# A chunked RWKV-7 recurrence with a hash-routed expert layer: the first group's triangular inverse in 16-row blocks

## The chip, the cores and the metric

The kernel runs on one core of a Trainium2 chip. The metric is the device time of one execution in microseconds. Before the change three runs took 639.33, 641.83 and 646.64 us, median 641.83.

A core has five engines that run at the same time, each through its own list of instructions and in order: TensorE (PE in the profile, with PEld for its weight loads), VectorE (DVE), ScalarE (ACT), GpSimd (POOL) and SyncE (SP). TensorE writes its results to eight banks of PSUM, from which VectorE and ScalarE copy them to SBUF. SP, POOL and ACT issue DMA transfers.

## The reference

There are two parts. The first is a recurrence over 768 steps for each of 4 x 8 heads, with a 40 x 40 state for each head:

```python
for t in range(S):
    y[:, :, t] = np.einsum('bhd,bhde->bhe', rt, state)
    Sa = np.einsum('bhde,bhe->bhd', state, at)
    state_decay = state * wt[:, :, None, :] - np.einsum('bhd,bhe->bhde', Sa, bt)
    state = state_decay + np.einsum('bhd,bhe->bhde', vt, kt)
```

The state starts at zero. The second part takes y as 3072 rows of 320 and sends each row through one of 8 experts, chosen by a hash of the row's token: `np.maximum(xe @ w1[e], 0.0) @ w2[e]`. All is in float32.

## The kernel before

The recurrence is worked out in chunks of 64 steps. A tile is one chunk of two of the four batches (16 heads), and there are 24 tiles. Inside a chunk the steps depend on one another through a strictly triangular 64 x 64 matrix for each head, built from a, b and the decays; the kernel inverts (identity minus this matrix) explicitly. For each tile u there are two halves.

- The scores (`tile_a`), at tick u. VectorE multiplies a, b and k with products of decays (`at`, `z`), TensorE turns these (`z_ps`, `t_ps`) and multiplies them (`a_ps`). VectorE masks one half of `a_ps` (`mk`). ScalarE copies the other half: the two 32 x 32 blocks on the diagonal to `pk`, the block beside them to `no`.
- The state step (`tile_s`, `tile_m`, `tile_b`), eight ticks later (`LAG`). It takes the inverse (`um`), the state and v to the new rows (`r1_ps`, `nc_ps`, `x_t_ps`, `rc_ps`), the next state (`s_ps`, `sd_ps`) and the output (`y_ps`).

In between, four tiles make a group, and `group_i` inverts the 32 x 32 blocks of the whole group at once on VectorE, with the elements of 128 matrices on 128 partitions. After a transpose (L613) come 30 steps, one for each column: a product into `outer` (L632) and its sum into `nu` (L639), of 32 to 272 elements on each partition, each needing the one before. Two transposes (L647, L648) bring the result back as `ut` and `ug`. `tile_m` then makes each tile's 64 x 64 inverse from the two inverted blocks: TensorE multiplies `no` with one of them (`x_ps`), ScalarE copies it and the blocks themselves (`xi`, `um`), TensorE multiplies with the other (`u_ps`), and ScalarE copies that to its place.

The decays come in six rounds of four tiles each (`decays`): products over w by levels on VectorE (L384, then `spread`, L393 and L395), stored to DRAM through SP's queue (L355) as p and q, and loaded again for each tile through POOL's queue (`ql`, `pl`).

The order on every engine is written out by hand. Each piece of work has a place on a scale of ticks (`at_tick`), and the list is sorted by it; inside a tick 14 steps have names (`STEPS`). The program then waits wherever data or buffers need it. For the scores of tiles 4 to 6 `LATE` gives fractions of a tick by which they come later. All matmuls go through one helper, L307, so the profile names them by their tiles. PSUM is shared by six buffers: four of one bank (`bank`) and two of two banks (`two_banks`); `z_ps`, `a_ps`, `nc_ps`, `x_t_ps`, `rc_ps` and `sd_ps` all take turns on the two.

The states live in three forms: `st`, and two copies of it in the layouts that the products need (`sb` and `sd`), filled with zeros by ScalarE at ticks 4.2, 4.9 and 5.9 and written after every state step.

## Time and profile before

One execution was profiled. It took 640.76 us, of which the profile spans 638.6.

| engine | busy us | share of the span |
|---|---|---|
| PE | 558.6 | 87% |
| PEld | 424.1 | 66% |
| DVE | 352.2 | 55% |
| ACT | 295.5 | 46% |
| POOL | 196.0 | 31% |

The recurrence takes about the first half: `a_ps` of the last tile starts at 303 us. The rest is the expert layer, which the change does not touch. Of the recurrence, the first 88 us build up: the decays of rounds 0 to 2, the scores of tiles 0 to 7 and the inversion of the first group. Then the state steps begin, and each later tick is one tile's scores with another tile's state step.

A line of a timeline has the start, the length from the first start to the last end, the engine, the line of the program, the operation, what it writes and reads, its shape and how many instructions are merged; in brackets stands how long the engine was idle before it and what ended that. A line of a table by stage has the window, its length, and then busy time and number of instructions of PE, PEld, DVE, ACT and POOL, TensorE's granted clock (1.00 is full speed), the DMA engines' mean busy share, and GB/s.

### The profile page before, as it was taken

To read this page: it belongs to the slowest core of one execution; us is meant where nothing else is said; L and a number is where in the kernel's file an instruction comes from. 1 tells how busy PE (TensorE), PEld (TensorE's weight loads), DVE (VectorE), ACT (ScalarE), POOL (GpSimd) and SP (SyncE) were. 2 spreads that over 40 slices of the span, in tenths; PEclk is the share of its full clock that TensorE was granted. 3 is DMA by queue.
4 is the path that set the end of the run, shared out by engine and by line. 5 is a ranking of instruction groups with operands and counts; after the bars stand their busy time and mean duration, and the time that the engine had idled before them with its cause. 6 is when DMAs were issued, how large, how long until landed. Compare 5 with 4: busy or idle time off the path is not lost.

```text
span 638.6 us, 22953 instructions
## 1 busy us (share of the span) xinstructions
PE 558.6 (87%) x9866; PEld 424.1 (66%) x9866; DVE 352.2 (55%) x920; ACT 295.5 (46%) x695; POOL 196.0 (31%) x331
## 2 busy tenths in 40 slices
PE   0443678899989999999999998999999999999995
PEld 0432667788878887888888887756565646565552
DVE  6878879768968986887797443132022112303010
ACT  4162457667767877778675751014042213101110
POOL 0621351425333345333231321461313132130101
PEclk9985579899999999999999999999999999999998
DMA  9999997978898797732435614695334273220000
GB/s 160 192 205 170 178 180 120 192 136 156 177 159 153 138 184 151 134 87 58 107 67 113 148 45 147 198 329 192 111 104 132 96 259 106 88 82 12 31 12 25
DMA packets 195769, 85.12 MB, mean 133 GB/s; under 512 B 176718, under 2 KB 186191, under 8 KB 195664
## 3 DMA queue, kind: packets, MB, share of 16 engines
q1 hardware_dynamic: 184016, 45.59, 37.5%
q0 software_dynamic: 11456, 37.37, 20.3%
q8 instruction: 78, 1.28, 0.8%
q10 hardware_dynamic: 192, 0.66, 0.4%
q14 instruction: 27, 0.22, 0.1%
HBM read 66.54 MB, written 15.40 MB: 128 GB/s over the span
## 4 chain that ended last, share of the span: by engine, by line
PE 42%; issue 22%; DVE 16%; DMA 5%; SPq 5%; POOL 4%; ACT 4%; POOLq 0%; DVEq 0%; ACTq 0%
PE up_ps L1077 6%; PE dn_ps L1095 6%; PE y_ps L307 4%; PE s_ps L307 3%; PE rc_ps L307 3%; SPq L326 3%; PE a_ps L307 3%; DVE mr L762 3%; PE x_t_ps L750 2%; DVE outer L632 2%; POOL out_dram L1100 2%; PE sd_ps L810 2%; DVE nu L639 2%; PE nc_ps L307 2%; PE x_ps L307 2%
## 5 line engine op out<-in xcount | busy, mean ns | idle before, releaser
L1085 DVE TENSOR_SCALAR ht<-up_ps 128x416 f32<-128x416 f32 (+2 forms) x36 | 19.4, 543 | 165.1 <-PE up_ps L1082 163.5
L1095 PE MATMUL dn_ps<-w,ht 128*128 128x320 f32 x336 | 91.7, 433 | 0.0
L1077 PE MATMUL up_ps<-xt,w 128*128 128x416 f32 x224 | 81.3, 516 | 0.0
L1095 PEld LDWEIGHTS dn_ps<-w,ht 128*128 128x128 f32 x336 | 63.3, 190 | 25.5
L1100 POOL DMA_INDIRECT out_dram<-o,idx_all x26 | 26.1, 1004 | 166.3 <-ACT o L1099 164.8
L802 POOL DMA_DIRECT2D x_rows<-xs x44 | 23.2, 535 | 164.5 <-DVE xs L798 56.9
L1087 ACT ACTIVATE ht<-up_ps 128x416 f32<-128x416 f32 (+2 forms) x36 | 17.2, 479 | 107.4 <-PE up_ps L1082 107.4
L1077 PEld LDWEIGHTS up_ps<-xt,w 128*128 128x128 f32 x224 | 41.9, 190 | 36.9 <-issue 31.7
L632 DVE TENSOR_TENSOR outer<-nu 128x252 f32<-128x252 f32 (+8 forms) x180 | 63.5, 353 | 5.3
L639 DVE TENSOR_TENSOR nu<-nu,outer 128x252 f32<-128x252 f32 (+8 forms) x180 | 63.2, 351 | 4.6
L1099 ACT COPY o<-dn_ps 128x320 f32<-128x320 f32 x26 | 11.1, 426 | 92.5 <-PE dn_ps L1095 92.5
L537 PE MATMUL z_ps<-ident,z 128*104 128x128 f32 x192 | 31.9, 319 | 20.0 <-DVE z L523 17.2
L541 ACT COPY z_t<-z_ps 104x512 f32<-104x512 f32 x48 | 25.8, 590 | 38.8 <-PE z_ps L537 37.6
L740 ACT COPY x<-nc_ps 64x320 f32<-64x320 f32 x48 | 20.2, 420 | 50.5 <-PE nc_ps L307 49.9
L484 POOL DMA_DIRECT2D ql<-q_rows x48 | 25.1, 531 | 50.0 <-DVE pb L393 15.8
L537 PEld LDWEIGHTS z_ps<-ident,z 128*104 128x104 f32 x192 | 25.1, 152 | 22.8 <-issue 18.8
L762 DVE TENSOR_TENSOR mr<-rc_ps,after 128x1024 f32<-128x1024 f32 x24 | 29.3, 1219 | 13.3 <-PE rc_ps L307 13.3
L307 PE MATMUL rc_ps<-r_t,x_t 64*64 64x64 f32 x1536 | 29.6, 222 | 7.4 <-DVE mk L564 4.3
L307 PE MATMUL a_ps<-at_t,z_t 64*64 64x64 f32 x1536 | 31.5, 237 | 3.6 <-ACT at_t L590 2.7
L307 PEld LDWEIGHTS rc_ps<-r_t,x_t 64*64 64x64 f32 x1536 | 25.5, 134 | 12.5 <-DVE mk L564 8.8
L564 DVE TENSOR_TENSOR mk<-a_ps,after 128x512 f32<-128x512 f32 x24 | 16.5, 689 | 30.7 <-ACT no L581 26.6
L307 PEld LDWEIGHTS a_ps<-at_t,z_t 64*64 64x64 f32 x1536 | 27.9, 149 | 6.4 <-ACT at_t L590 3.9
(230 smaller groups left out, 1127.8 us busy)
## 6 DMA issues: line engine op xcount, KB each, us to landing
ql<-q_rows POOLq DMA_DIRECT2D x48, 160.0 KB, 4.1
w<-in_moe_w_dram SPq DMA_DIRECT2D x10, 640.0 KB, 7.4
w<-in_moe_w_dram SPq DMA_DIRECT2D x10, 512.0 KB, 4.7
al<-in_a_dram SPq DMA_DIRECT2D x48, 80.0 KB, 4.4
pl<-p_rows POOLq DMA_DIRECT2D x48, 80.0 KB, 4.5
r<-in_r_dram SPq DMA_DIRECT2D x48, 80.0 KB, 3.6
x<-in_v_dram SPq DMA_DIRECT2D x48, 80.0 KB, 3.2
py<-p_rows POOLq DMA_DIRECT2D x48, 80.0 KB, 4.3
```

Of the source, the lines that this page charges most:

```text
L307: nc.tensor.matmul(out_, lhsT=lhsT, rhs=rhs, start=start, stop=stop, skip_group_check=True)
L484: nc.gpsimd.dma_start(ql[half(be)], of_batches(rows_of_chunk("q"), 2 * g, 2))
L537: nc.tensor.transpose(p[0:R, be, hp * P:(hp + 1) * P], x["z"][:, be, hp, :], ident[:])
L541: nc.scalar.copy(t[0:R, be].rearrange("p h t -> p (h t)"), p[0:R, be])
L632: nc.vector.tensor_tensor(tv, paired(x["u"])[:, 0:full[1], j:j + 1, :].to_broadcast(full), paired(x["n"])[:, j // 2, j + 1:, j % 2].unsque ...
L639: nc.vector.tensor_tensor(o, o, x["t"][:, 0:n].rearrange("p (c i k) -> p c i k", c=full[1], k=2), op=OP.add)
L740: nc.scalar.copy(x["x"][half(be), be].rearrange("p (a q) (two e) -> p a (q two) e", a=2, two=2)[:, :, :, 0:D], p[half(be), :, 0:HP * D].re ...
L762: nc.vector.tensor_tensor(t[:].rearrange("p two h t -> p (two h) t"), p[:].rearrange("p two (h t) -> p (two h) t", t=C), after[:].unsqueez ...
L802: dma(x_of[2 * g + be, n * C:(n + 1) * C], xs[half(be), :])
L1077: nc.tensor.matmul(p[:], lhsT=w1[c][:, (f0 + i) * P:(f0 + i + 1) * P], rhs=xt[:, c, 0:n], start=(c == 0), stop=False)
L1095: nc.tensor.matmul(p[i * m:(i + 1) * m], lhsT=ht[:, f, c0:c0 + m], rhs=w2[f // (FP // 2)][:, f % (FP // 2), :], start=(f == 0), stop=(f == ...
L1100: st = nc.gpsimd.indirect_dma_start(out=out[:], out_offset=bass.IndirectOffsetOnAxis(ap=idx, axis=0), in_=o[0:m], in_offset=None, bounds_c ...
```

## The change

For the first group alone, the explicit inversion on VectorE goes by blocks of 16 rows: 14 steps, not 30, each of two products (one for each of two pairs of blocks) and one sum. The rest of each 64 x 64 matrix, that is the three 16-row strips beside the four inverted blocks, is kept whole in `off` (a fill and three scaled copies by ScalarE, in place of the copy `no`). `tile_m16` takes the place of `tile_m` for tiles 0 to 3. It multiplies `off` with the inverted blocks on TensorE (`mt_ps`), copies that to `mt` and the blocks to `um`, and then forms um + mt x now three times in series, now being um first and then the last result: each time one product with the identity, 16 products of 64 x 64 and a copy by ScalarE (`sum_ps`). These pieces stand at ticks 5.3, 6.12 and 6.92 for tiles 0 to 2 and 10.22 for tile 3, with 0.2 ticks between them.

`off` and, for tiles 0 and 1, `um` are kept in the buffers of `sb` and `sd`, which are cleared later (ticks 7.55 to 10.3). Since these states are empty in the first chunk, the products with them (`r1_ps` and `y_ps` for tiles 0 and 1) are left out. The buffer of `mt` is one of the two of `wt`, the loaded decays. The places of tiles 4 to 6's scores move later, and so do the spreads and stores of the decays of round 2 and the load of round 3. In the sorted order this puts, on TensorE, the products of tile 0 between `z_ps` and `a_ps` of tile 5, those of tile 1 before `a_ps` of tile 6, and those of tile 2 before `a_ps` of tile 7; on VectorE the spreads of round 2 come behind the inversion of group 0; on SP the stores of round 2 and the load of round 3 come directly before the first loads of r and v and before the loads of tile 8. The other groups are inverted as before, by the same code under a new name (`by_columns`).

The diff, cut to its core:

```diff
-    sb_r, sd_r = (ring(n, NG, [P, 2, HP, 2, D], all_of, i) for n, i in (("sb", 4.9), ("sd", 5.9)))
+    states = [hold.tile([P, 2, HP, 2, D], F32, name=f"s{n}{i}") for n in "bd" for i in range(NG)]
+    sb_r, sd_r = ((lambda u, ts=ts: ts[u % NG]) for ts in (states[:NG], states[NG:]))
+    for i, t in enumerate(states):
+        at_tick((8.25, 9.25, 7.55, 10.3)[i])(lambda t=t: clear(t[:]))
+    def lent(u):
+        return states[u][:].rearrange("p b hp two d -> p (b hp two d)")[:, 0:HP * 2 * C].rearrange("p (h t) -> p h t", t=C)
...
+    HB = BLK // 2
+    above = hold.tile([P, 3], F32, name="above")
+    nc.vector.memset(above[:], 0.0)
+    for be in range(2):
+        for i in range(3):
+            nc.vector.memset(above[be * C:be * C + (i + 1) * HB, i:i + 1], 1.0)
...
-    LATE = {4: 0.45, 5: 0.3, 6: 0.15}
+    LATE = {4: 0.6, 5: 0.4, 6: 0.2}
...
-            x["no"] = no = work.tile([P, 2, HP, BLK], F32, tag="no", name="no", bufs=LAG)
+            if not ahead:
+                x["no"] = no = work.tile([P, 2, HP, BLK], F32, tag="no", name="no", bufs=LAG)
             nc.scalar.copy(pk, of_k(of_b[:, :, :, 0:BLK]))
             for i in range(2):
                 nc.scalar.copy(pk[low(i)], of_k(of_b[low(i), :, :, BLK:C]))
-            nc.scalar.copy(no[:], of_b[:, :, :, BLK:C])
+            if not ahead:
+                nc.scalar.copy(no[:], of_b[:, :, :, BLK:C])
+            else:
+                x["off"] = off = lent(u)
+                nc.scalar.copy(off[:, :, 0:HB], zero[:].unsqueeze(1).to_broadcast([P, H, HB]))
+                for i in range(3):
+                    cols = slice((i + 1) * HB, (i + 2) * HB)
+                    nc.scalar.activation(off[:, :, cols].rearrange("p (two h) t -> p two h t", two=2), of_b[:, :, :, cols],
+                                         AF.Copy, scale=above[:, i:i + 1])
...
+        if gi == 0:
+            dt = (t2 - t1) / (2 * HB - 3)
+            def sub(v, row, col, dims, q=None):
+                step = HB // 2 * 2 * BLK + HB * 2
+                return bass.AP(v.tensor, v.offset + row // 2 * 2 * BLK + col * 2 + row % 2 + (q or 0) * step,
+                               [v.ap[0], *([(step, 2)] if q is None else []), *dims])
+            @at_tick(t1, order=9)
+            def _():
+                nc.vector.tensor_copy(sub(x["u"], 0, 1, [(2, HB - 1)]), sub(x["n"], 0, 1, [(2, HB - 1)]))
+            for j in range(1, HB - 1):
+                m, c = HB - 1 - j, j // 2 + 1
+                @at_tick(t1 + dt * (2 * j - 1), order=9)
+                def _(j=j, m=m, c=c):
+                    x["t"] = work.tile([P, BLK * BLK // 4 + BLK // 2], F32, tag="outer", name="outer", bufs=1)
+                    tv = x["t"][:, 0:4 * c * m].rearrange("p (q c i k) -> p q c i k", q=2, c=c, k=2)
+                    for q in range(2):
+                        nc.vector.tensor_tensor(tv[:, q], sub(x["u"], 0, j, [(2 * BLK, c), (0, m), (1, 2)], q),
+                                                sub(x["n"], j, j + 1, [(0, c), (2, m), (0, 2)], q), op=OP.mult)
+                @at_tick(t1 + dt * 2 * j, order=9)
+                def _(j=j, m=m, c=c):
+                    o = sub(x["u"], 0, j + 1, [(2 * BLK, c), (1, 2 * m)])
+                    tv = x["t"][:, 0:4 * c * m].rearrange("p (q c i) -> p q c i", q=2, c=c)
+                    nc.vector.tensor_tensor(o, o, tv, op=OP.add)
+        else:
+            by_columns(x, t1, t2)
...
+    def mt_buffer():
+        groups[0]["mt"] = early.tile([P, HC * D], F32, tag="wt", name="mt", bufs=2)[:, 0:4 * HP * C].rearrange(
+            "p (two h t) -> p two h t", two=2, t=C)
+    at_tick(8.9)(mt_buffer)
+    def tile_m16(u, t0):
+        x = tiles[u]
+        @at_tick(t0)
+        def _():
+            ut, ug = (paired(groups[0][n])[:, u * H // 2:(u + 1) * H // 2] for n in ("ut", "ug"))
+            if u == 0:
+                mt_buffer()
+            both = groups[0]["mt"]
+            x["mt"], x["sum"] = mt, _ = both[:, 0], both[:, 1]
+            p = two_banks("mt_ps")
+            for par, be, hp in heads_of("par", "be", "hq", "al"):
+                h, a = hx(par, be, hp), al(hp)
+                for i, rows in enumerate((top(a), low(a))):
+                    mm(p[half(a), i, h * BLK:(h + 1) * BLK], x["off"][rows, h, :], ut[rows, h // 2, :, h % 2])
+            nc.scalar.copy(mt.rearrange("p h (two t) -> p two h t", two=2),
+                           p[:, :, 0:H * BLK].rearrange("p two (h t) -> p two h t", t=BLK))
+            x["um"] = um = lent(u) if u < 2 else work.tile([P, H, C], F32, tag="um", name="um", bufs=1)[:]
+            for i in range(2):
+                nc.scalar.activation(um[:, :, i * BLK:(i + 1) * BLK].rearrange("p (g k) t -> p g k t", k=2),
+                                     ug.rearrange("p g t k -> p g k t"), AF.Copy, scale=first[:, i:i + 1])
+        for i, f in enumerate((0.2, 0.4, 0.6)):
+            @at_tick(t0 + f)
+            def _(i=i):
+                mt, um = x["mt"], x["um"]
+                now = x["sum"] if i else um
+                p = bank([P, H, C], "sum_ps")
+                mm(p.rearrange("p h t -> p (h t)"), ident[:], um.rearrange("p h t -> p (h t)"), stop=False)
+                for par, be, hp in heads_of("par", "be", "hq", "al"):
+                    h, a = hx(par, be, hp), al(hp)
+                    mm(p[half(a), h, :], mt[half(a), h, :], now[half(a), h, :], start=False)
+                nc.scalar.copy(um if i == 2 else x["sum"], p)
     def tile_m(u, t0):
 
         x = tiles[u]
         gi, ti = divmod(u, GRP)
         x_order = ("par", "be", "hq", "al")
+        if gi == 0:
+            return tile_m16(u, (5.3, 6.12, 6.92, 10.22)[u])
...
-            for _, be, hp in heads_of("hq", "be", "al"):
+            for _, be, hp in heads_of("hq", "be", "al") if n else ():
...
-            for _, be, hp in heads_of("hp", "be"):
+            for _, be, hp in heads_of("hp", "be") if n else ():
...
-    decays(2, 0.86, 2.7, 0.2, (3.0, 3.01, 3.02, 3.66, 3.67, 4.0, 4.3, 4.31))
+    decays(2, 0.86, 2.7, 0.2, (3.0, 3.01, 3.02, 5.26, 5.27, 5.4, 5.41, 5.42))
...
-        decays(ri, t0 - 2.1, t0, 0.12, [t0 + f for f in (0.86, 0.92, 0.921, 1.0, 1.3, 1.86, 2.0, 1.31)])
+        decays(ri, t0 - (1.5 if ri == 3 else 2.1), t0, 0.12, [t0 + f for f in (0.86, 0.92, 0.921, 1.0, 1.3, 1.86, 2.0, 1.31)])
...
-        group_i(gi, t0 + 0.05, t0 + (0.33 if last else 0.1), t0 + (3.44 if last else 3.4))
+        group_i(gi, t0 + 0.05, t0 + (0.33 if last else 0.1), t0 + (3.44 if last else 3.4 if gi else 1.6))
```

More of the change, by code (lines that the diff above doesn't have):

```diff
@@ L596, in paired, with by_columns, place_of @@
         return t.rearrange("p (i j k) -> p i j k", i=BLK // 2, k=2)
-    def group_i(gi, t0, t1, t2):
-        x = groups[gi]
-        @at_tick(t0 - 0.5, order=9)
-        def _():
-            x["nu"] = nu = early.tile([P, 2, BLK * BLK], F32, tag="nu", name="nu")
-            x["n"], x["u"] = nu[:, 0], nu[:, 1]
-            ub = x["u"]
-            nc.gpsimd.memset(ub, 0.0)
-            nc.gpsimd.memset(bass.AP(ub.tensor, ub.offset, [ub.ap[0], (2 * BLK + 4, BLK // 2), (3, 2)]), 1.0)
-        @at_tick(t0, order=9)
-        def _():
-            nc.vector.transpose(paired(x["n"]).rearrange("p s t k -> p t s k"), paired(x["pk"]).rearrange("p t h k -> p t k h"))
+    def by_columns(x, t1, t2):
         dt = (t2 - t1) / (2 * BLK - 3)
-        place_of = (lambda t: max(t1, by_time(t))) if gi else (lambda t: t)
+        def place_of(t):
+            return max(t1, by_time(t))
         @at_tick(t1, order=9)
@@ L639, in _, with group_i @@
                 nc.vector.tensor_tensor(o, o, x["t"][:, 0:n].rearrange("p (c i k) -> p c i k", c=full[1], k=2), op=OP.add)
-        @at_tick(place_of(t2), order=9)
+    def group_i(gi, t0, t1, t2):
+        x = groups[gi]
+        @at_tick(t0 - 0.5, order=9)
+        def _():
+            x["nu"] = nu = early.tile([P, 2, BLK * BLK], F32, tag="nu", name="nu")
+            x["n"], x["u"] = nu[:, 0], nu[:, 1]
+            ub = x["u"]
+            nc.gpsimd.memset(ub, 0.0)
+            nc.gpsimd.memset(bass.AP(ub.tensor, ub.offset, [ub.ap[0], (2 * BLK + 4, BLK // 2), (3, 2)]), 1.0)
+        @at_tick(t0, order=9)
+        def _():
+            nc.vector.transpose(paired(x["n"]).rearrange("p s t k -> p t s k"), paired(x["pk"]).rearrange("p t h k -> p t k h"))
+        if gi == 0:
[5 more added lines that the diff above has]
+            @at_tick(t1, order=9)
+            def _():
+                nc.vector.tensor_copy(sub(x["u"], 0, 1, [(2, HB - 1)]), sub(x["n"], 0, 1, [(2, HB - 1)]))
[15 more added lines that the diff above has]
+            by_columns(x, t1, t2)
+        @at_tick(max(t1, by_time(t2)) if gi else t2, order=9)
@@ L648, in _ @@
             nc.vector.transpose(paired(ug).rearrange("p g t k -> p t g k"), ub.rearrange("p s t k -> p t s k"))
+    def mt_buffer():
[5 more added lines that the diff above has]
+        @at_tick(t0)
+        def _():
+            ut, ug = (paired(groups[0][n])[:, u * H // 2:(u + 1) * H // 2] for n in ("ut", "ug"))
[25 more added lines that the diff above has]
+                nc.scalar.copy(um if i == 2 else x["sum"], p)
     def tile_m(u, t0):
@@ L725, in _ @@
                 mm(p[half(al(hp)), par, hp % HQ * 2:hp % HQ * 2 + 2, :], x["mk"][:, par, hp, :], x["x"][:, :, hp, par * C:par * C + D],
-                   start=False)
+                   start=n == 0 and par == 0 and hp % HQ == 0)
             x["r1"] = r1 = r1_r(u)
@@ L795, in _ @@
                 mm(p[half(be), c0:c0 + D], x["mr"][:, par, hp * 2 + be, :], x["z"][:, be, hp, par * C:par * C + D],
-                   start=False)
+                   start=n == 0 and par == 0 and hp == 0)
             xs = work.tile([P, DM], F32, tag="xs", name="xs")
```

## The prediction

> **What bounds the kernel now.** I read the busy shares in 40 slices first, then the engines by stage, then the timelines of VectorE, TensorE and ScalarE from 25 to 145 us, and the chain of waits for the same time. The change touches only the first group, so the question is what sets the pace before the loop of tiles is full.
>
> ```profile
> PE   0443678899989999999999998999999999999995
> DVE  6878879768968986887797443132022112303010
> PEclk9985579899999999999999999999999999999998
> ```
>
> A slice is 16 us. In slices 3 to 5 TensorE (PE) is half idle at a low clock and VectorE (DVE) is full; from slice 6 on TensorE is full. By stage (busy us, then the clock and the DMA share):
>
> ```profile
> 57.70:67.20 9.50, 4.76 (x76) 4.18 (x76) 8.09 (x19) 4.29 (x10) 3.09 (x6) 0.50 0.96 165
> 98.10:112.40 14.30, 12.49 (x376) 10.77 (x370) 13.78 (x33) 10.16 (x25) 1.99 (x5) 1.00 0.77 128
> 130.50:143.10 12.60, 12.48 (x374) 10.87 (x370) 9.94 (x27) 9.50 (x23) 2.26 (x4) 1.00 0.71 117
> ```
>
> The third number group is VectorE: 8.1 of 9.5 us while group 0 is inverted, 13.8 of 14.3 while group 1 is, and 9.9 of 12.6 later, where TensorE (first group) is the full one. The exact borders come from the timelines. VectorE:
>
> ```profile
> 46.81 1.24 DVE L613 STREAM_TRANSPOSE nu<-pk 128x1024 f32<-128x1024 f32 x1
> ...
> 81.62 1.25 DVE L647 STREAM_TRANSPOSE ut<-nu 128x1024 f32<-128x1024 f32 x1
> ...
> 90.05 0.69 DVE L564 TENSOR_TENSOR mk<-a_ps,after 128x512 f32<-128x512 f32 x1 [2.48 <-ACT no L581]
> 90.66 1.24 DVE L613 STREAM_TRANSPOSE nu<-pk 128x1024 f32<-128x1024 f32 x1
> ...
> 115.82 0.68 DVE L564 TENSOR_TENSOR mk<-a_ps,after 128x512 f32<-128x512 f32 x1
> ```
>
> Group 0 takes VectorE from 46.8 to 84.0. The scores of tiles 4 to 7 lie inside it; those of tile 7 end at 88.4 and its mask at 90.66. There group 1 begins, and from 90.66 to the mask of tile 9 (116.4) VectorE has no listed wait: 25.8 us that its own order sets. After that TensorE sets the pace to the end of the loop. So one number carries the forecast: **when tile 7's mask is done**, 90.66 now. All behind it moves with it.
>
> **What goes.** Of group 0's 60 column operations (L632, L639; in all 63.5 + 63.2 us over six groups, 21.1 for one, 22.9 with 0.03 between two) 42 small ones stay. Rows: 60 elements take 0.22, 272 take 0.44, so about 0.16 + 0.001 an element; two independent ones overlap by 0.08 (L384: 0.48 long, 0.39 apart). A step has two products of 16 to 72 elements and one sum of twice that: 0.13 + 0.25 + 0.305 = 0.69 on average, 14 steps 9.6 us. Bounds: 14 x 3 x 0.19 (the smallest row) = 8.0 and, without overlap, 11.3. VectorE saves about 13 us. Also gone for tiles 0 to 3 are x_ps, u_ps and their copies, r1's state half and y's state half for tiles 0 and 1 (0.77 each), and one 0.37 copy "no" per tile.
>
> **What comes on ScalarE and VectorE early.** "no" becomes a fill and three scaled copies of 128x128: between 0.25 and 0.35 each by the 0.30 apart of 128x192 copies (L205); I take 0.26, so +0.7 a tile. Each a_ps buffer is free that much later; two of these lie on the chain, and mk of tile 3 goes from 44.07 to 45.5. But the 2.1 us of L393 between it and the transpose move behind the inversion, so the transpose needs only tile 3's pk copies: 47.4 against 46.81. Inversion begins at 49.05; six steps 4.2; at and z of tile 4 1.15 (their data landed by 52.3); eight steps 5.4: 59.8. at and z of tile 5 follow, to 61.0. Tile 4's scores on cold TensorE: z_ps 54.5, t_ps, a_ps 58.05 to 60.05; copies 1.55, mk to 62.35. Then the ut transposes, the first done at **63.6 against 82.9**. That is the gain: 19 us.
>
> **What is put in its place.** TensorE is in order, and the products of tile 0 stand before a_ps of tile 5, those of tile 1 before a_ps of 6, those of tile 2 before a_ps of 7. So the saved time does not reach tile 7 unless the products are short. Rows for them:
>
> ```profile
> 96.12 0.70 PE L307 MATMUL s_ps<-st,ident 104*104 104x320 f32 x2
> 96.75 0.81 PE L307 MATMUL s_ps<-x,z 128*40 128x40 f32 x32
> 97.50 0.69 PE L307 MATMUL u_ps<-um,xi 32*32 32x32 f32 x32
> 98.12 1.16 PE L307 MATMUL a_ps<-at_t,z_t 64*64 64x64 f32 x64
> ```
>
> The identity product has 512 columns: 0.63 x 512/320 = 1.0 us. Its 16 products of 64x64 are half of a_ps: 0.57 (0.69 by u_ps). One stage **1.57 us** at full clock, bounds 1.46 (up_ps has 0.87 ns a column) and 1.81. Behind each stage is a ScalarE copy of 128x512 with handover, 0.65, which the next one needs: three in series, nothing of the same tile beside them. mt_ps is 32 products, 64 records: 64/32 x 0.69 = 1.38, bounds 1.16 (a_ps) and 2.26 (y_ps, 1.13 for 32). Copy 0.6 and um 0.95 (L669) must end before the first stage.
>
> mt_ps also needs a two-bank buffer. There are two: z_ps of the next tile takes one, and the other is a_ps of the tile before, free after its mask. So one tile runs, from the end of an a_ps: 1.65 for pk and no, 0.7 mk, 1.4 mt_ps, 0.6 + 0.95, 3 x 1.57 + 2 x 0.65 = 6.0, some 0.1 in handovers, a_ps 1.16: **12.55 us**. z_ps and t_ps lie in its gaps. Now it is 9.2 to 10 (a_ps at 57.7, 67.2, 76.4, 86.4), even at half clock.
>
> Sum: mt_ps of tile 0 63.65 to 65.75 (cold, 2.1), um done 67.3, first stage 2.4 while the clock rises, 69.75; second 71.95; third 74.2; a_ps of tile 5 ends 75.35. Two cycles of 12.55: a_ps of tile 7 ends at 100.45, its mask 2.3 later (as now): **102.75 against 90.66, +12.1 us**.
>
> **Behind it.** Group 1's 25.8 us on VectorE keep the same operations in the same order, so TensorE's savings there (x, u and r1's half, 2 to 3 us) are not seen. After tile 9's mask TensorE leads:
>
> ```profile
> 120.83 0.66 PE L307 MATMUL nc_ps<-r,um 64*64 64x40 f32 x28
> 123.12 0.44 PE L307 MATMUL nc_ps<-r,um 64*64 64x40 f32 x4 [1.63 <-issue]
> 123.49 1.06 PE L307 MATMUL x_ps<-ut,no 32*32 32x32 f32 x32
> ```
>
> There TensorE stops 1.63 us and then runs at half clock until 129: with the durations of the next tick nc to a_ps would be 4.9 us, not 9.05. Tile 3's mt_ps and stages come in just here: mt 1.24, wait for um 0.85, sum 1.57, x_t and s 2.25, sum 1.57 and sd in between make 8.2 from nc's end, third stage 1.57 after a_ps. If the stop does not come back this tick ends 0.7 later than now; if it does, up to 4.5 more. Total **+12.8**: 640.76 + 12.8 = 653.6, so **654**. The profiled execution (span 638.6, 2.2 around it) is 1.1 under the median 641.83 of runs from 639.33 to 646.64, and I leave it there.
>
> **Transfers.** Round 2's stores (4.2 and 5.6 us on SP) move from 60 to behind the inversion, and round 3's w behind them. Issued from about 67 they end near 77; w and r, v and tile 8's loads follow to 87. Tile 8's z is due only after tile 6's mask, near 94, so this costs nothing; without the long TensorE chain it would be up to 10 us late, another reason why a fast chain would not give its whole gain. The states are filled later on ScalarE, 0.7 each, beside TensorE's work: nothing. Round 4's w now waits for round 3's and holds SP's queue (r, v and q stores behind it) some 5 us; r_t there is due 13 us later, so nothing, at worst 5.
>
> **The clock, weighed apart.** In the row, 1.6 us of stop at 121.5 is enough for 0.50 from 123 on, and 4.7 us of work (76.4 to 81.1) lift it. The Trainium skill (TensorE: Matmul & The Clock Gate, "What's actually happening") says that the clock falls after an idle window of about 3.4 us; by it the chain, whose gaps are 0.65 to 1.3, stays warm, and the sum is the 654 above; by the row it may fall in each tile.
>
> **Rivals.** (1) *Forecast*, 650 to 657: 0.50. (2) *The gaps cool TensorE*: busy only 9 of 12.5 us. All cold a cycle is 2.35 + 2.1 + 1.55 + 9 + 1.3 + 2 = 18.3, a_ps of tile 5 ends 79.65, tile 7's mask 118.6: 669. Half of it 661. For it: 0.50 all through 45 to 80; against it: 32 to 44, warm at 55% busy. 0.25 for 657 to 669. (3) *Cheaper by its own bounds or a gain behind it* (TensorE's savings seen after all, up to 3; mt at 1.16; stages at 1.46; mk earlier): 645 to 650: 0.15. (4) *Not slower*: one mechanism, the price of a product stage. Twelve of them lie on the path (nine before tile 7, three in tile 3's tick); 12.8/12 = 1.07, so at 0.5 us or less instead of 1.57 the change is level, about 641, and below it faster. Against it: no row has 512 columns in less than 0.89. 0.08, and 0.02 for anything above. (5) *The small blocks save nothing*, since operations have a fixed cost: at worst 11.3 instead of 9.6, +1.7: inside (1).
>
> Of (4), half is faster by over 1%; 1% (6.4 us) is about what can be told from no change: some of (3) lies within it. Faster 0.04, same 0.11, slower 0.85. Range 645 to 664: it leaves out the coldest part of (2) and (4).
>
> **What would show it.** Right: ut transpose near 64; a_ps of tiles 5, 6, 7 more than 11 us apart, with three waits of TensorE on ScalarE's sum copies in each; tile 7's mask past 100; then 25 to 26 us to tile 9's. Wrong: stages below 1 us, or a clock of 0.5 in the chain (then nearer 661), or mt_ps not waiting for mk.

## The result and the profile after

The changed kernel takes 661.59 us (median of 4 runs, 657.83 to 663.2) against 641.41 us (639.33 to 646.64) for the kernel before in the same session: a ratio of 1.0294, 95% interval 1.0218 to 1.0369. It is slower, by some 14 to 24 us. The profiled execution took 657.83 us, its span is 656.0; before it was 640.76 and 638.6, so the two executions that are compared below differ by 17.1. The profiled one is the fastest of the four, and the medians differ by 20.2: some 3 us of the loss are in no trace.

The busy shares in 40 slices (of 16.4 us each) of the kernel after:

```profile
PE   0444888789999999999999998999999999999995
...
DVE  6858424975897898887798653133020302213010
...
PEclk9985879899999999999999999999999999999998
```

Counted from 0, VectorE's slices 4 to 6 fell from 8, 7, 9 to 4, 2, 4: the inversion did get short. TensorE's (PE) slices 4 to 6 rose from 6, 7, 8 to 8, 8, 8, and its busy time over the whole span from 558.6 to 577.6 us. What VectorE does with its free time stands in its timeline (start, length, line, operation; in brackets the idle time before it and what ended that):

```profile
48.94 1.25 DVE L666 STREAM_TRANSPOSE nu<-pk 128x1024 f32<-128x1024 f32 x1 [1.22 <-ACT pk L596]
...
63.73 1.24 DVE L707 STREAM_TRANSPOSE ut<-nu 128x1024 f32<-128x1024 f32 x1
...
79.08 0.69 DVE L579 TENSOR_TENSOR mk<-a_ps,after 128x512 f32<-128x512 f32 x1 [7.62 <-ACT no L598]
...
94.43 0.69 DVE L579 TENSOR_TENSOR mk<-a_ps,after 128x512 f32<-128x512 f32 x1 [13.53 <-ACT no L598]
...
107.08 0.69 DVE L579 TENSOR_TENSOR mk<-a_ps,after 128x512 f32<-128x512 f32 x1 [8.35 <-ACT no L598]
107.69 1.24 DVE L666 STREAM_TRANSPOSE nu<-pk 128x1024 f32<-128x1024 f32 x1
...
132.88 0.68 DVE L579 TENSOR_TENSOR mk<-a_ps,after 128x512 f32<-128x512 f32 x1
```

The inverse of group 0 comes back (L707) from 63.73 on, and came from 81.62 (L647 before). Then VectorE waits 7.6, 13.5 and 8.4 us for the scores of tiles 5, 6 and 7. The releaser that the profile names, ScalarE's copy `no`, only stands behind `a_ps` of these tiles, and that stands on TensorE behind the new products. Group 1's first transpose starts at 107.69; before at 90.66. From it to tile 9's mask it is 25.19 us, and was 25.16. So what is lost is lost ahead of 107.69.

TensorE's timeline after, the products of tile 1 and the beginning of those of tile 2. Each stage is an identity product (128x512) and 16 products of 64x64 (32 records):

```profile
79.82 1.13 PE L322 MATMUL mt_ps<-ut,sb 32*64 32x32 f32 x64 [1.39 <-DVE mk L579]
...
82.49 2.08 PE L322 MATMUL sum_ps<-sb,ident 128*128 128x512 f32 x2 [0.95 <-ACT sb L738]
84.50 1.97 PE L322 MATMUL sum_ps<-sb,mt 64*64 64x64 f32 x32
86.40 2.07 PE L322 MATMUL sum_ps<-sb,ident 128*128 128x512 f32 x2
88.40 1.30 PE L322 MATMUL sum_ps<-mt 64*64 64x64 f32 x32
89.63 1.12 PE L322 MATMUL sum_ps<-sb,ident 128*128 128x512 f32 x2
...
97.85 1.12 PE L322 MATMUL sum_ps<-um,ident 128*128 128x512 f32 x2 [0.95 <-ACT um L738]
98.90 1.15 PE L322 MATMUL sum_ps<-um,mt 64*64 64x64 f32 x32
```

Two things are to be seen. The same pair of operations takes 4.0 us in tile 1's first stage and 2.2 in tile 2's. And inside a tile no line after the first identity product has a wait: TensorE never stops for ScalarE's copy of the sum. The table by stage says why the first is so long; the windows are one tile each (from `a_ps` to `a_ps`; tiles 5 to 6, the cold part of it, 6 to 7) and then group 1's part (window, length, busy us of PE, PEld, DVE, ACT, POOL, TensorE's granted clock, DMA share, GB/s):

```profile
76.32:91.67 15.35, 13.01 (x253) 8.46 (x251) 1.82 (x3) 6.11 (x13) 8.29 (x16) 0.78 1.03 196
82.49:88.40 5.91, 5.91 (x36) 2.78 (x36) 0.00 (x0) 1.01 (x2) 4.21 (x9) 0.50 1.16 210
91.67:104.15 12.48, 10.13 (x252) 7.13 (x250) 4.16 (x12) 6.12 (x13) 3.06 (x6) 1.00 0.76 136
107.69:132.88 25.19, 18.53 (x445) 15.08 (x444) 23.85 (x63) 15.80 (x38) 5.97 (x12) 0.93 0.59 116
```

At full clock a tile takes 12.48 us, with half the clock for 5.9 us of it 15.35; before it was 9.2 to 10. The time is lost in three such tiles.

### The profile page after: what moved, and what is told of

Read it like the earlier page. It is cut to its first block, busy times and chain, and to the rows that moved or that the text cites. A ratio compares the mean times of both kernels' runs of the same rounds, so it can differ in the third digit from the quotient of the medians.

```text
span 656.0 us, 23646 instructions
## 1 busy us (share of the span) xinstructions
PE 577.6 (88%) x10210; PEld 432.1 (66%) x10210; DVE 340.4 (52%) x909; ACT 301.3 (46%) x707; POOL 195.8 (30%) x331
## 4 chain that ended last, share of the span: by engine, by line
PE 45%; issue 22%; DVE 15%; ACT 7%; POOL 4%; SPq 4%; DMA 2%; POOLq 0%; DVEq 0%; ACTq 0%
PE up_ps L1182 6%; PE dn_ps L1200 6%; PE sum_ps L322 5%; PE y_ps L322 4%; PE a_ps L322 3%; DVE mr L867 3%; SPq L341 3%; PE s_ps L322 3%; DVE outer L642 2%; POOL out_dram L1205 2%; PE rc_ps L322 2%; DVE nu L649 2%; PE x_t_ps L855 2%; PE nc_ps L322 2%; DVE mk L579 2%
## 5 line engine op out<-in xcount | busy, mean ns | idle before, releaser
L1192 ACT ACTIVATE ht<-up_ps 128x416 f32<-128x416 f32 (+2 forms) x36 | 17.2, 478 | 107.5 <-PE up_ps L1187 107.4
L642 DVE TENSOR_TENSOR outer<-nu 128x252 f32<-128x252 f32 (+8 forms) x150 | 53.0, 353 | 4.3
L649 DVE TENSOR_TENSOR nu<-nu,outer 128x252 f32<-128x252 f32 (+8 forms) x150 | 52.7, 351 | 3.7
L552 PE MATMUL z_ps<-ident,z 128*104 128x128 f32 x192 | 29.5, 302 | 14.2 <-DVE z L538 11.1
L552 PEld LDWEIGHTS z_ps<-ident,z 128*104 128x104 f32 x192 | 23.2, 143 | 16.8 <-issue 10.4
L322 PEld LDWEIGHTS rc_ps<-r_t,x_t 64*64 64x64 f32 x1536 | 25.8, 136 | 12.5 <-DVE mk L579 7.6
L797 POOL MEMSET x<- 64x512 f32 x48 | 25.1, 524 | 19.8 <-ACT x_t L857 13.5
```

What stands on the lines that cost most here:

```text
L322: nc.tensor.matmul(out_, lhsT=lhsT, rhs=rhs, start=start, stop=stop, skip_group_check=True)
L552: nc.tensor.transpose(p[0:R, be, hp * P:(hp + 1) * P], x["z"][:, be, hp, :], ident[:])
L642: nc.vector.tensor_tensor(tv, paired(x["u"])[:, 0:full[1], j:j + 1, :].to_broadcast(full), paired(x["n"])[:, j // 2, j + 1:, j % 2].unsque ...
L649: nc.vector.tensor_tensor(o, o, x["t"][:, 0:n].rearrange("p (c i k) -> p c i k", c=full[1], k=2), op=OP.add)
L797: nc.gpsimd.memset(x["x"][half(be), be], 0.0)
```

## The experiments

All of them are read by the same marks: where group 1's transposes start, where `a_ps` of tile 11 starts (from there TensorE has the same order in all kernels, and the rest takes 493.7 to 498.2 us in all of them), and the span. Each mark is read from one execution. The 143.11 of the kernel before holds a stop of TensorE of 1.63 us with half clock behind it; the two kernels at the end of the table, which take as long as it, have 140.0 and 140.7. So differences of up to 3 us at that mark say little.

| kernel | transposes of group 1 | a_ps of tile 11 | span | time, or ratio to before |
|---|---|---|---|---|
| before | 90.66 | 143.11 | 638.6 | 641.41 |
| after | 107.69 | 162.06 | 656.0 | 1.0294 (1.0218 to 1.0369) |
| one stage of three | 94.52 | 148.91 | 646.4 | 648.14 (one run) |
| fillers in the gaps | 104.70 | 159.08 | 657.1 | 658.91 (one run) |
| products of tiles 1 and 2 in the loop | 91.00 | 158.43 | 653.9 | 1.0222 (1.0169 to 1.0276) |
| the same without identity products | 92.35 | 155.67 | 651.8 | 653.55 (one run) |
| no products | 92.97 | 143.87 | 638.3 | 640.15 (one run) |
| no products, round 2's stores at the old places | 91.70 | 140.59 | 638.2 | 639.99 (one run) |
| no products, no stores of round 2 | 85.84 | 133.95 | 631.4 | 0.9869 (0.9808 to 0.993) |
| before without the stores of round 2 | 90.51 | 139.64 | 633.3 | 0.9952 (0.9922 to 0.9983) |
| before, moved places alone | 90.26 | 141.43 | 638.1 | 640.27 (one run) |
| before, empty states left out | 91.48 | 140.04 | 635.9 | 1.0018 (0.999 to 1.0046) |
| before, both of the last two | 92.47 | 140.67 | 638.9 | 0.9997 (0.9965 to 1.0028) |

The single runs are to be held against the runs of before that were made beside them: 643.66 (median) for one stage, the fillers and no products, 642.21 for the others.

My theory was the one of the prediction: the products in series ahead of tile 7's scores are the loss, by their number and their clock, and if they were cheap enough the kernel would gain. The rival was that something else would have held tile 7's mask in their place.

**One stage of three**, for tiles 0 to 2. It leaves out two of the three terms of these tiles' inverses.

```diff
         for i, f in enumerate((0.2, 0.4, 0.6)):
+            if u < 3 and i < 2:
+                continue
```

> The changed kernel with one product stage instead of three for tiles 0 to 2, tile 3 as it was. Two of the three terms of these tiles' sums are left out, so the result is not the reference's. Theory: each stage of 2.1 us (at full clock) stands on the path to tile 7's scores, so six fewer take 12.8 us off, and some 2 to 3 more if the cold spell in tile 6's stages goes with them: tile 7's mask at 92 to 95 instead of 107.7, span 640 to 644. Rival, transfers or VectorE set tile 7: mask stays past 102, span above 650.

Tile 7's mask was done and the transposes began at 94.52, in the range; 6 stages less brought 13.2 us. Of these 1.0 lies ahead of the products (the blocks came back at 62.70, not 63.73), and the clock fell here too (0.66 from tile 5 to 6); 12.1 are left, 2.0 for each stage. `a_ps` of tile 11 came 13.2 us earlier too. At the end 9.6 of the span are left (646.4, where 640 to 644 was expected): TensorE's stops without a listed wait fell otherwise (one of 1.97 us at 196). The time follows the number of stages.

**Fillers in the gaps**: matmuls of no use on a bank of their own, four ahead of each `mt_ps` and three ahead of each first stage of tiles 0 to 2.

```diff
+    def warm(n):
+        p = bank([P, P], "warm")
+        for _ in range(n):
+            mm(p, ident[:], ones[:])
...
+            if u < 3:
+                warm(4)
...
+                if i == 0 and u < 3:
+                    warm(3)
                 p = bank([P, H, C], "sum_ps")
```

> The changed kernel with idle-time matmuls added on TensorE: four of 128 columns before each mt_ps of tiles 0 to 2 and three before their first product stage, into a PSUM bank that nobody reads. Nothing is left out. Theory: the clock fell to half at 82 us because of the gaps of 1.4 and 0.95 us in front of tile 1's stages, and that cost 2.8 us (a_ps of 5 to 6: 15.35 us, of 6 to 7: 12.5 us). Filled, both distances are 12.5 and tile 7's mask comes at 104 to 105; span 653. Rival, the clock falls for another reason or at random: distances as before or the cold spell elsewhere, span 656 or, since the added matmuls take their time when cold, up to 659.

TensorE, tile 1:

```profile
79.69 1.13 PE L322 MATMUL mt_ps<-ut,sb 32*64 32x32 f32 x64 [0.51 <-DVE mk L579]
...
82.36 1.12 PE L322 MATMUL sum_ps<-sb,ident 128*128 128x512 f32 x2 [0.28 <-ACT sb L745]
83.42 1.15 PE L322 MATMUL sum_ps<-sb,mt 64*64 64x64 f32 x32
```

With gaps of 0.51 and 0.28 us in place of 1.39 and 0.95 the first stage takes 2.2 us, not 4.0; the tiles are 12.5 us apart both times, and the transposes began at 104.70, 3.0 us earlier, as expected. So tile 1's half clock was 2.8 us of the 17; the other 14 stay with the chain at full clock from there on. The gain is not seen in the span (657.1, expected 653): stops of TensorE without a listed wait of 1.4, 0.9, 0.7 and 0.6 us followed later, where "after" has one of 1.1. A single run can't tell whether these belong to the edit.

**Products of tiles 1 and 2 in the loop**, where those of tile 3 are, so that only tile 0's stand ahead of tile 7's scores.

```diff
-        at_tick((8.25, 9.25, 7.55, 10.3)[i])(lambda t=t: clear(t[:]))
+        at_tick((8.25, 9.25, 9.3, 10.3)[i])(lambda t=t: clear(t[:]))
-            return tile_m16(u, (5.3, 6.12, 6.92, 10.22)[u])
+            return tile_m16(u, (5.3, 8.22, 9.22, 10.22)[u])
```

> The changed kernel with the products of tiles 1 and 2 moved from before the scores of tiles 6 and 7 into the loop (ticks 8.22 and 9.22, as tile 3's stand at 10.22); the state buffer lent to tile 2 is cleared later. Theory: the products in TensorE's order are what makes tile 7 late (a_ps of 5, 6, 7 end at 77.4, 92.8, 105.2 us). Without them a_ps of 6 and 7 follow 5 within 5 us each; tile 7's mask then waits for tile 8's loads (VectorE has z of tile 8 before it), so it comes near 92 instead of 107.7. In ticks 8 and 9 TensorE gets 12 us more work where VectorE now sets 25 us, so 5 come back: the profiled span near 646 (656.0 in the changed kernel). Rival A, TensorE's total work decides and the place does not: 654 to 657. Rival B, the transfers (stores of round 2 before tile 8's loads) decide: mask near 100 or later and z of tile 8 waiting for a DMA.

The transposes came at 91.00, 16.7 us earlier, as early as before. But only 3.6 us of it reached tile 11. VectorE up to tile 7's mask, and then the loop by stage (from `a_ps` of tile 8 to that of tile 9, and on to tile 10):

```profile
81.25 0.49 DVE L399 TENSOR_TENSOR pb<-wt 128x320 f32<-128x320 f32 x1 [1.45 <-DMA wt<-in_w_dram]
...
87.29 0.49 DVE L531 SCALAR_TENSOR_TENSOR at<-al,pl 128x320 f32<-128x320 f32 x1 [3.54 <-DMA al<-in_a_dram]
89.66 0.83 DVE L538 TENSOR_TENSOR z<-kb,ql 128x640 f32<-128x640 f32 x1 [1.88 <-DMA kb<-in_k_dram]
90.40 0.68 DVE L579 TENSOR_TENSOR mk<-a_ps,after 128x512 f32<-128x512 f32 x1
```

```profile
106.59:125.02 18.43, 17.18 (x451) 13.23 (x449) 13.05 (x30) 12.15 (x25) 5.20 (x10) 1.00 0.86 170
125.02:144.14 19.12, 18.14 (x467) 13.98 (x465) 10.21 (x26) 11.54 (x24) 5.19 (x10) 1.00 0.65 114
```

In the loop TensorE is busy 17.2 of 18.4 us at full clock: there the products cost their full time, some 6 us a tick over the 12.5 of a tick without them. The first rival is right on this (span 653.9; my theory had 646). The other fence shows something that neither theory had in its sum: VectorE, free at last, waits 6.9 us for loads of the next decays and of tile 8 (`al`, `kb`). Tile 7's mask stands behind these operations on VectorE, though `a_ps` of tile 7 was done at 81.8.

**The same without identity products**: um is added by one sum on VectorE and one on GpSimd, and the second and third product are left in one bank.

```diff
...
-                mm(p.rearrange("p h t -> p (h t)"), ident[:], um.rearrange("p h t -> p (h t)"), stop=False)
...
-                    mm(p[half(a), h, :], mt[half(a), h, :], now[half(a), h, :], start=False)
-                nc.scalar.copy(um if i == 2 else x["sum"], p)
+                    mm(p[half(a), h, :], mt[half(a), h, :], now[half(a), h, :], start=i != 1)
+                if i < 2:
+                    nc.scalar.copy(x["sum"], p)
+                if i == 0:
+                    nc.gpsimd.tensor_tensor(um, um, x["sum"], op=OP.add)
...
+            nc.vector.tensor_tensor(x["um"], x["um"], x.pop("sum_ps"), op=OP.add)
```

> As the run with the products of tiles 1 and 2 in the loop, and each set of products cut without leaving a term out: the identity products go; the second stage adds onto the first one's bank, ScalarE copies after the first two stages, GpSimd adds the first to um, VectorE adds the third. TensorE has 3.2 us less for each tile (three identity products of 1.05). Theory: in the loop TensorE's total sets the pace (tile 11's scores at 158.4 with the identity products), so three sets save 9 and tile 0's chain some more that the transfers hide: 148 to 151. Rival, the series of copies sets it: 155 or later.

In the loop nine identity products of 1.05 us were taken out, and 2.8 us came of it at tile 11. Tile 8's z came late again (TensorE idle 5.7 us, then half clock until 104), and two stops of 0.7 and 1.2 us without a listed wait, half clock behind the second, fell into the ticks. So even cheaper products leave the kernel slow. The number is the rival's; its cause, the series of copies, is not shown: in the ticks TensorE waits for ScalarE's `um` (1.2 us twice), and not for the copies between the stages.

**No products**: for tiles 0 to 3 neither `mt_ps` nor the stages are made. It leaves the products out, so that um holds the inverted blocks alone. This is the change with its products at no price at all.

> The changed kernel without any of the new products: no mt_ps and no product stages for tiles 0 to 3; their inverse holds only the blocks on the diagonal, so the result is not the reference's. It shows what the 16-row inversion is worth if the rest cost nothing. Theory: a_ps of tiles 5 to 7 follow each other in 5 to 6 us and are done by 80; z of tile 8 then waits for its loads (about 91), so the mask of tile 7 comes near 92, about where it is before the change, and the early end of the inversion (65 against 84) buys almost nothing there; tile 3's tick loses 6 us and the span is 634 to 637 (before: 638.6). Rival, nothing but the products holds tile 7: mask near 84 and span near 627.

VectorE again:

```profile
82.52 0.49 DVE L399 TENSOR_TENSOR pb<-wt 128x320 f32<-128x320 f32 x1 [2.53 <-DMA wt<-in_w_dram]
...
89.14 0.49 DVE L531 SCALAR_TENSOR_TENSOR at<-al,pl 128x320 f32<-128x320 f32 x1 [4.12 <-DMA al<-in_a_dram]
91.63 0.83 DVE L538 TENSOR_TENSOR z<-kb,ql 128x640 f32<-128x640 f32 x1 [2.00 <-DMA kb<-in_k_dram]
```

`a_ps` of tile 7 ends at 83.1, against 88.4 before, but the transposes begin at 92.97 (expected near 92), 2.3 us later than before, after 8.7 us of waits for transfers. `a_ps` of tile 11 is level with before (143.87 and 143.11), and so is the span (638.3, where 634 to 637 was expected). The 18 us by which the blocks are ready earlier are worth nothing at tile 7's mask, even where the products cost nothing. Over the whole, one run of 640.15 beside seven of the kernel before, 641.18 to 644.22, leaves room for some 3 us and not for 18.

**What holds these loads?** First the spreads and stores of round 2's decays back at their old places, still without products (the products are left out as above):

```diff
-    decays(2, 0.86, 2.7, 0.2, (3.0, 3.01, 3.02, 5.26, 5.27, 5.4, 5.41, 5.42))
+    decays(2, 0.86, 2.7, 0.2, (3.0, 3.01, 3.02, 3.66, 3.67, 4.0, 4.3, 4.31))
```

> As the run without any products (the inverse holds only the diagonal blocks), with the spreads and stores of round 2 put back to their places before the change. Theory: there VectorE waited for tile 8's a, b and k (mask of tile 7 at 92.4 though its scores ended at 83.1), because round 2's stores stand before these loads in SP's queue. With the stores earlier the mask comes at 86 to 88 and tile 11's scores near 138 (143.9 there), span 632 to 635. Rival, the loads come no earlier since the transfers are limited by their total: 92 and 144.

91.70: the place of the stores is not it. VectorE waited 4.1, 1.9 and 3.1 us for the same three loads. SP's timeline shows where they stand; first the kernel before, then this one:

```profile
73.40 3.09 SPq L370 DMA_DIRECT2D wt<-in_w_dram  x4
76.53 1.29 SPq L326 DMA_DIRECT2D al<-in_a_dram  x2
77.86 1.32 SPq L326 DMA_DIRECT2D kb<-in_b_dram  x2
79.23 2.44 SPq L326 DMA_DIRECT2D kb<-in_k_dram  x2
```

```profile
77.11 1.28 SPq L341 DMA_DIRECT2D r<-in_r_dram  x2
78.44 1.32 SPq L341 DMA_DIRECT2D x<-in_v_dram  x2
80.49 3.48 SPq L341 DMA_DIRECT2D al<-in_a_dram  x2
84.07 2.17 SPq L341 DMA_DIRECT2D kb<-in_b_dram  x2
86.28 1.31 SPq L341 DMA_DIRECT2D kb<-in_k_dram  x2
```

From 30 us on SP's issues have one gap of 1.4 us in the kernel before and none above 0.8 us here. In the kernel before tile 8's `kb` is issued by 81.67, and z uses it at 86.75 without a wait, a landing later (2.9 us at the least): by this estimate just in time. Here the first r and v (2.7 us) stand ahead of it, as in the kernel after, the issues themselves take longer, and it is out only at 87.6. Turning r and v back behind `kb` alone wasn't tried; it could give up to those 2.7 us. Then no stores of round 2 at all; its tiles load the rows of round 1 in their place, so that their decays are those of other steps:

```diff
-            for y in range(2 * RN):
+            for y in range(2 * RN) if ri != 2 else ():
...
+    pq_dram[2] = pq_dram[1]
```

> As the run without products for tiles 0 to 3, and besides without the stores of the decays of round 2 (8 x 160 KB on SP's queue; the tiles of round 2 load the rows of round 1 in their place). There the scores of tile 7 were done at 83.1, but VectorE then waited for the loads of tile 8 and the transposes of group 1 began at 92.97. Theory (the total of the early transfers, not their order, holds tile 8's loads): with 1.28 MB fewer to move, some 7 us at the 175 GB/s of that time, the transposes begin at 85 to 87. Rival (these loads wait for something else, a buffer or SP's order): 90 or later.

```profile
82.56 0.49 DVE L532 SCALAR_TENSOR_TENSOR at<-al,pl 128x320 f32<-128x320 f32 x1
82.97 0.82 DVE L539 TENSOR_TENSOR z<-kb,ql 128x640 f32<-128x640 f32 x1
85.23 0.69 DVE L580 TENSOR_TENSOR mk<-a_ps,after 128x512 f32<-128x512 f32 x1 [1.45 <-ACT no L599]
85.84 1.23 DVE L667 STREAM_TRANSPOSE nu<-pk 128x1024 f32<-128x1024 f32 x1
```

The three waits are gone, the mask follows the scores, the transposes begin at 85.84, 7.1 us earlier than without products alone, and the whole kernel is at 0.9869. So without products the early transfers that stand ahead of tile 8's loads are the limit. The 7.1 us are what the next limit leaves, the scores behind ScalarE's copy (1.45 us of wait): tile 8's last `kb` was issued by 75.51 here and by 88.21 there. Whether it is SP, whose eight stores took 7.05 us to issue in the run without products, or the DMA engines, which need 7.3 us for 1.28 MB at 175 GB/s, these runs don't tell. The same edit in the kernel before:

> The kernel before, without the same stores of round 2 (its tiles load the rows of round 1). Theory (there VectorE's inversion of group 0, which ends at 84.0, and the transfers end within a few us of each other): the inversion stays, tile 7's mask is ready some 6 us after it as now, and the transposes of group 1 begin at 89.5 to 91. Rival (transfers alone set it): 85 to 87.

There the mark doesn't move: 90.51. VectorE's own inversion ends at 83.8 and sets the rest. (By the profiled execution the 0.9952 comes from behind this mark; what of it is the missing traffic there and what the stop of 1.63 us at 121, which was absent, is open.) The kernel before has two limits close together: 90.51 with the inversion alone, 90.66 with both, and 91.70 to 92.97 where only the transfers are left (with r and v ahead of tile 8's loads). Taking away one alone leaves the other. The DMA engines' share (last but one number) in the kernel before, while this goes on:

```profile
30.00:40.00 10.00, 7.24 (x221) 6.00 (x219) 6.01 (x13) 7.88 (x21) 1.06 (x3) 1.00 1.05 185
50.00:60.00 10.00, 4.97 (x77) 4.34 (x77) 9.38 (x25) 3.47 (x10) 2.21 (x5) 0.50 1.09 182
80.00:90.00 10.00, 6.42 (x148) 5.39 (x148) 7.23 (x18) 5.46 (x15) 5.42 (x11) 0.67 0.93 159
```

In all six windows of 10 us from 30 to 90 the share is 0.93 to 1.09, at 158 to 227 GB/s.

**The parts that are not products.** The moved places alone, in the kernel before:

```diff
-    LATE = {4: 0.45, 5: 0.3, 6: 0.15}
+    LATE = {4: 0.6, 5: 0.4, 6: 0.2}
-    decays(2, 0.86, 2.7, 0.2, (3.0, 3.01, 3.02, 3.66, 3.67, 4.0, 4.3, 4.31))
+    decays(2, 0.86, 2.7, 0.2, (3.0, 3.01, 3.02, 5.26, 5.27, 5.4, 5.41, 5.42))
```

(and round 3's load at 1.5 ticks, not 2.1, ahead of its products)

> The kernel before with the change's places alone: the spreads and stores of round 2 behind group 0's inversion, round 3's load and the scores of tiles 4 to 6 later. The inversion itself is as before. Theory: SP's queue then has 13 us of stores and round 3's w between the inversion and tile 8's loads; VectorE has z of tile 8 before tile 7's mask, so the mask comes near 100 instead of 90.7 and tile 11's scores near 152. Rival, the places are neutral: 143.

I had expected about 100 here, with the spreads behind the long inversion; it was 90.26, and the rival is right. VectorE did wait 3.1 us for tile 8's `kb`, until 88.92, but tile 7's mask waits for ScalarE's copies until 89.0 in any case.

The empty states left out, in the kernel before, once and then, the same kernel, in twelve runs:

> The kernel before with one part of the change alone: the products with the empty states are left out for tiles 0 and 1. Read at the start of tile 11's scores (143.1 us before, 162.1 changed). Theory: of the four products of 0.77 us three lie where VectorE sets the pace (90.7 to 116.4) or before it waits anyway, so at most 0.8 us is gained: 142.3 to 143.2. Rival, TensorE sets the pace there after all: 140 to 141.

> The kernel before with only the empty states left out: the products of r1 and y with the states of tiles 0 and 1 are not made. In its one look it spanned 637.5 against 638.6, and a_ps of tile 11 began 3.2 us earlier. Theory (the removed products lie in ticks that VectorE's inversion of group 1 sets, and what follows is the wandering of TensorE's own stops): no difference that can be measured, ratio 0.995 to 1.000. Rival (the 1.63 us stop of TensorE and its half clock are avoided for good): 3 us kept to the end, ratio 0.992 to 0.996, interval below 1.

The first execution had `a_ps` of tile 11 at 139.89, 3.2 us earlier than before, where the 1.63 us stop of TensorE at 121 and its half clock were not there, and a time of 639.62. In 12 runs against 22 the ratio is 1.0018 (0.999 to 1.0046): nothing. The stop is not tied to these products. And both together:

> The kernel before with the empty states left out and with the changed places alone (spreads and stores of round 2, load of round 3, scores of tiles 4 to 6), that is the change without 16-row blocks and without the products in series. Theory (neither part moves the transposes of group 1, near 90.5, since tile 8's loads can't land before about 87): ratio 0.993 to 1.000, no difference that can be measured, and the whole +17 us of the change comes from the blocks' products. Rival (the places cost something together with the rest): ratio above 1.005.

0.9997 (0.9965 to 1.0028). What is left of the change, the blocks with their products and the copies and buffers that go with them, makes the whole difference. No kernel that computes everything beats the kernel before by more than the runs differ.

## Why the prediction was right, and where it was off

Forecast 654 with a range of 645 to 664, measured 661.59: slower, and in the range, but 7.6 us above the likeliest value. In the two profiled executions +12.8 was forecast and +17.1 measured; what follows explains these 4.3 us, and not the 3 us more between the medians.

- **What bounds the kernel: tile 7's mask.** Right. Of +17.1, +17.0 are there (transposes at 107.69 against 90.66); +0.03 over group 1 on VectorE, as forecast; +1.9 from there to `a_ps` of tile 11, forecast +0.7; -1.6 in the rest of the span, -0.3 around it.
- **VectorE's gain.** 14 steps were put at 9.6 us and took 9.2 (50.57 to 60.88 without at and z, 1.14). The result came back 1.4 us later than forecast (first transpose done at 64.97, not 63.6), nearly all from the start: 48.94, not 47.4. Of these 1.5 us 1.1 are the clock's: behind a gap of 3.23 us `f_ps` and `a_ps` of tile 3 ran at half clock, 0.65 and 1.99 us. In the kernel before they took 0.41 and 1.16 us behind a gap of the same length.
- **A stage: sum right, parts wrong.** I took 1.57 of products and 0.65 of ScalarE's copy in series, 2.22. Measured: 2.13 a stage, with no wait for the copy. The identity product is 1.05 (forecast 1.0); the 16 products are 1.08, not 0.57; the copy (0.58 at 72.27) lies beside the next identity product, which reads only um. "Three in series, nothing of the same tile beside them" was wrong, the three waits for the copies that were to be seen in each tile did not come, and by luck two errors of 0.5 to 0.65 us cancelled. I had taken half of `a_ps`'s 64 records. In `a_ps` they work in all four quarters of the array, 17 to 18 ns a record; the products lie in the two quarters on the diagonal, 34 ns a record. That this place is the reason was not tried by itself. In the loop, where other work already hides the copy, only the error of the products is left, 0.5 us in each of three stages: that is enough for the difference of +1.9 and +0.7.
- **The cycle of a tile.** 12.55 forecast; 12.48 measured where the clock was full (tile 6 to 7). The two-bank buffer makes `mt_ps` wait for the mask as I said: it starts 2.40 us after the end of `a_ps` (1.65 and 0.7 forecast), and um adds a wait of 0.95.
- **The clock: the step that failed.** The forecast held the chain warm. It was cold longer than forecast in tile 0's first stage (3.6 us, forecast 2.4), and again in tile 1's first and half of its second (0.50 from 82.5 to 88.4): of the 4.9 us between 102.75 and 107.69 2.8 are tile 1's, and 2.1 the beginning's, from `a_ps` of tile 3 and this first stage. So the second rival happened in one tile of three, and the profiled execution lies between it and the forecast. The median is in that rival's range (657 to 669, chance 0.25) and above the forecast's (650 to 657, chance 0.50), and the sign of being wrong that went with it, a clock of 0.5 in the chain and a time nearer 661, came: the stated range held because it took in half of this rival. With the gaps filled tile 1 stayed at full clock; that the gaps alone cool it is not shown, since tile 2's did not. I had weighed the Trainium skill's figure of about 3.4 us of idle (TensorE: Matmul & The Clock Gate, "What's actually happening") against a row with 1.6 us, and taken the page; here half clock followed gaps of 1.39 and 0.95 us once. The same page warns of it in another place ("A second HAM failure mode: psum-queue depth-cycling"): short idle times between groups of matmuls can make the clock go up and down too. In this chain it went down in one tile of three, which had such gaps, and not in the next, which had them too.
- **Transfers.** The stores moved at no cost: right (0.9997 with the moved places). "Up to 10 us late without the long chain": right in size, 8.7 us of waits were measured without products. The reason was not the place of the stores: with them at their old places the waits were 9.2 us. And I left this out of the fourth rival, which put the level point at 0.5 us a stage and "faster" below it. Without any product the kernel is level, within some 3 us. The chance of "faster" should have been smaller still, and the argument for it was already in my text.

## What to carry to other kernels

Work that is made cheaper on the busiest engine is worth only what lies before the next limit, and a build-up phase can have several that end within 2 to 3 us of each other: read the DMA share and the issuing queue of the same stretch, and ask when the next data could land at all, before a price is set on the engine's gain. Work that is moved to another engine costs there twice: in series in the build-up, and at full price in the loop if that engine is what sets the loop. For small products, price a record by a row with the same place in the array, not only the same size. And a row shows what the clock did in one execution; the same program can run the same stage at half clock in the next.

## What the runs showed of the hardware

- The same gaps did not always cool TensorE, not even in one program. Ahead of `a_ps` of tile 3 TensorE is idle for 3.23 us in all 14 profiled executions; in 10 of them half clock follows (`a_ps` 1.99 us), in 4 it does not (1.16 us; the kernel before is one). The kernel with the empty states left out was profiled twice and did both (the first `f_ps` at full clock, the second at half):

```profile
42.49 0.42 PE L400 MATMUL f_ps<-own,partner 128*128 128x40 f32 x2 [3.23 <-DVE own L381]
```

```profile
42.28 0.65 PE L400 MATMUL f_ps<-own,partner 128*128 128x40 f32 x2 [3.23 <-DVE own L381]
```

- Nor did shorter gaps always cool it. Windows of 3.4 us in the kernel after, around tile 1's and tile 2's first stages (columns as above):

```profile
79.70:83.10 3.40, 2.33 (x69) 1.94 (x70) 1.20 (x3) 2.21 (x5) 2.81 (x7) 0.83 1.03 231
83.10:86.50 3.40, 3.40 (x35) 1.89 (x33) 0.00 (x0) 0.00 (x0) 3.40 (x7) 0.50 1.12 225
...
93.30:96.70 3.40, 2.00 (x73) 1.67 (x71) 2.20 (x6) 2.37 (x6) 0.00 (x0) 1.00 0.53 81
96.70:100.10 3.40, 2.45 (x37) 1.43 (x36) 1.96 (x7) 1.57 (x5) 1.07 (x3) 1.00 0.57 90
```

  Tile 1's gaps of 1.39 and 0.95 us led to 0.50 with TensorE busy 2.33 of 3.40; tile 2's gaps of 1.40 and 0.95 did not, with 2.00 and 2.45. Once down, the clock stayed down for 5.9 us of unbroken work. A free-running window of some 3.4 us, of which the Trainium skill speaks (TensorE: Matmul & The Clock Gate, "What's actually happening"), would make the outcome depend on where the gap falls in it. That one program did both agrees with this; that half clock followed a gap of 3.23 us and shorter ones does not fit an idle window of 3.4 us, and the runs don't show the window. What differs beside it between tile 1 and tile 2 is the DMA traffic, 225 to 231 GB/s against 81 to 90; that this plays a part was not tried.
- TensorE's stops that the profile puts down to nothing ("issue", 0.15 to 2.0 us) fall at other places in every kernel, and half clock can follow them. The traces show what goes with them: packets of 16 KB on a DMA queue of kind "instruction" (q8), one for every 253 of TensorE's 19732 instructions in the kernel before, some 4.6 to 4.9 us apart. All 92 such stops between 85 and 310 us in the 14 profiles end 2.2 to 3.4 us after the start of such a packet; the stop of 1.63 us ends at 123.12, and its packet starts at 120.38. So TensorE seems to wait there for its next instructions; that was not tried. The stops move single executions by 1 to 3 us: the empty states seemed to gain 3.2 us at tile 11 in one and gained nothing in 12.
- The early transfers of the kernel before, from 30 to 90 us, run at a DMA share of 0.93 to 1.09 with 158 to 227 GB/s; in the kernel after, 44067 of 45092 packets between 30 and 100 us are under 512 bytes. Leaving out 1.28 MB of stores (7.05 us of issues) let SP issue tile 8's loads 12.7 us earlier without products, and moved the mark that hung on them by 7.1 us, to where the scores hold it.
